# Expert order, the place of the split of x, and the copy of gather indices in a fused attention and MoE kernel

## The chip, the cores and the metric

One core of a Trainium2 chip runs the whole kernel as one program. The time is device time of one execution in microseconds (us).

## The reference

Attention with a compressive memory gives 2304 rows of 512 numbers (4 batches, 8 heads, 576 positions, head width 64). A mixture of experts with one expert for each row follows. What is computed, in short:

```python
local = softmax(causal(q @ k.T / 8)) @ v
mem_out = (phi(q) @ M_prev) / (phi(q) @ z_prev + 1e-6)        # phi(x) = elu(x) + 1
x = rows(g * mem_out + (1 - g) * local)                       # g = sigmoid(beta), 2304 x 512
logits = x @ w_gate                                           # 8 experts
expert_idx = argmax(logits, axis=1)                           # the first one of equal logits
gate_w = softmax(logits)[arange(2304), expert_idx]
for e in range(8):
    xe = x[expert_idx == e]
    out[expert_idx == e] = gate_w[...] * (relu(xe @ w1[e]) @ w2[e])   # 512 -> 1024 -> 512
```

## The kernel before

The program has two parts. The attention part (to about 262 us) writes the rows x with their gates to a scratch tensor in HBM; its order is fixed by a planner with costs and due times (the table `K`). The routing then sorts the row numbers by expert: `idx` holds 128 row numbers for each slot, `cnt` the number of full slots and of all slots of each expert position.

The MoE part works through slots. A slot is up to 128 rows of one expert. A position whose last slot has at most 64 rows runs it as a half slot, with 64 columns instead of 128; every position has at least one slot. `weight_unit` says which expert stands at position p: here p ^ 1, so the order is 1, 0, 3, 2, 5, 4, 7, 6. The router's weights (`wg_sw`) and the tie-break weights (`w8`, from an index operation in `consts`) are put in the same order.

Weights come as fp32 in 512 KB units, eight to an expert, by SyncE's queue into two stages. ScalarE makes the high fp16 part of a unit (`conv_hi`), VectorE the low part (`conv_lo`), into one of three buffers (position modulo 3). The conversions of later positions are spread over the slots, four units to a slot; `cuts` says how many of VectorE's four lie behind the first relu and behind the second, the rest behind the copy of xT: (1, 2) in a full slot, (0, 1) in a half one.

In each slot TensorE multiplies xT with w1 in two halves (`first_part`, m_ph, 96 matmuls in all), then with w2 (`second_part`, m_py, 24 matmuls in a full slot, 48 in a half one). Its code is one loop: for each of the three weight buffers i there is a block F{i} for a full slot and H{i} for a half slot, laid out F0, H0, F1, H1, F2, H2 with a few branches behind each (L1652 to L1656; `following`). L1654 leads to a full block of the next buffer, L1656 to a half one.

The rows of a slot come in four steps: GpSimd copies a column of `idx` (L1537) and issues an indirect gather of 128 rows into `xg` (L1489); VectorE splits them into a high and a low fp16 part `xn` (L1779 and L1782); SyncE issues two transposing DMAs into `xB` (L1410); VectorE copies xB to `xT` (L1793) when TensorE has read the old xT. Slot 0 is prepared in the routing, slot 1 has a gather of its own (`xg0`, semaphore g0) and is turned by TensorE. In before, the split for slot k stands at the start of VectorE's slot k - 1, ahead of the relus (L1750, L1752). VectorE, ScalarE, GpSimd and SyncE have loops of their own with unrolled branches for each state of the conversions; all wait on semaphores against registers.

Of the kernel before, what the change touches and what calls it, by code (L numbers as in the profile page):

```python
# [11 lines left out]
ALU = mybir.AluOpType  # L12
# [64 lines left out]

def weight_unit(w1, w2, p, u):

    e = p ^ 1  # L80
    if u < 4:
        return w1[e, 128 * u:128 * u + 128, :]
    return w2[e, 256 * (u - 4):256 * (u - 4) + 256, :].rearrange("(f p) d -> p f d", p=128)
# [18 lines left out]
def attention(nc, tc, es, q, k, v, M_prev, z_prev, beta, wg, w1, w2, x_dram, logits, mem, rout=None):  # L102
# [69 lines left out]
    def setup():  # L172
        wg_sb = const.tile([128, 4, 8], F32, name="wg_sb")
        nc.sync.dma_start(out=wg_sb, in_=wg.rearrange("(c p) e -> p c e", p=128))
        bt = const.tile([128, 8], F32, name="bt")
        nc.sync.dma_start(out=bt, in_=beta.rearrange("(o h) -> o h", o=1).to_broadcast([128, 8]))

        gm = const.tile([128, 8], F32, name="gm")
        gl = const.tile([128, 8], F32, name="gl")
        nc.scalar.activation(out=bt, in_=bt, func=AF.Tanh, scale=0.5)  # L180
        nc.vector.tensor_scalar(out=gm, in0=bt, scalar1=0.5 * SX, scalar2=0.5 * SX, op0=ALU.mult, op1=ALU.add)
        nc.vector.tensor_scalar(out=gl, in0=bt, scalar1=-0.5 * SX, scalar2=0.5 * SX, op0=ALU.mult, op1=ALU.add)

        wg_in, wg_sb = wg_sb, const.tile([128, 4, 8], F32, name="wg_sw")
        for i in range(2):
            nc.vector.tensor_copy(out=wg_sb[:, :, i::2], in_=wg_in[:, :, 1 - i::2])
        IW = const.tile([128, 4, 2, 72], F32, name="IW")
        nc.gpsimd.memset(IW, 0.0)
        for hh in range(2):
            r = slice(64 * hh, 64 * hh + 64)  # L190
            nc.vector.tensor_copy(out=IW[r, :, hh, 0:64], in_=ident[r, 64 * hh:64 * hh + 64].unsqueeze(1).to_broadcast([64, 4, 64]))
            nc.vector.tensor_copy(out=IW[r, :, hh, 64:72], in_=wg_sb[r])
        mz = xp.tile([128, 32, 64], F32, tag="xb", name="mz")
        early = xp.tile([128, 512], F32, tag="xt", name="early")
        zt = early[0:32, 256:384].rearrange("p (a d) -> p a d", a=2)
        for hh in range(2):
            nc.sync.dma_start(out=zt[:, hh], in_=z_prev.rearrange("b h d -> (b h) d"))
        mh = const.tile([128, 32, 73], F16, name="mh")
        ml = const.tile([128, 32, 73], F16, name="ml")
        nc.gpsimd.memset(ml[64:128], 0.0)  # L200
        T["gm"] = gm
        mw = early[:, 0:256].rearrange("p (i e) -> p i e", e=8)
        wgp = early[:, 384:512].rearrange("p (c m) -> p c m", c=4)
        nc.gpsimd.memset(wgp, 0.0)
        for hh in range(2):
            nc.vector.tensor_copy(out=wgp[64 * hh:64 * hh + 64, :, 8 * hh:8 * hh + 8], in_=wg_sb[64 * hh:64 * hh + 64])
        mt = xp.tile([128, 32, 64], F32, tag="xb", name="mt2").rearrange("p a d -> p (a d)")
        T.update(IW=IW, gl=gl, mh=mh, ml=ml, mz=mz, mw=mw, zt=zt, wgp=wgp, pws=mt[:, 1024:1536].rearrange("p (b a d) -> p b a d", b=4, a=2),
                 mt=mt[:, 0:1024].rearrange("p (c b d) -> p c b d", c=4, b=4))
# [769 lines left out]
NE = 8  # L979
# [9 lines left out]
class Routing:  # L989
# [25 lines left out]
    def consts(s):  # L1015
        V, G, kp = s.nc.vector, s.nc.gpsimd, s.tc.keep_in_program_order
        kp(G.memset(s.tri, 1.0))
        kp(G.affine_select(out=s.tri, in_=s.tri, pattern=[[1, 128]], compare_op=ALU.is_gt, fill=0.0, base=0, channel_multiplier=-1))
        kp(G.memset(s.ones, 1.0))
        kp(G.memset(s.cnt[:, NE:], 0))  # L1020
        kp(G.memset(s.idx[:, NS:NS + 1], 2303))
        kp(G.memset(s.ids[:, NS:NS + 1], 2304))
        ii = s.idx[:, 0:NS]
        it = s.tmp
        kp(G.iota(ii, pattern=[[128, NS]], base=0, channel_multiplier=0))
        kp(V.tensor_scalar(out=s.col, in0=ii, scalar1=BIG, scalar2=None, op0=ALU.add))
        kp(G.iota(it, pattern=[[-1, 128]], base=0, channel_multiplier=0))
        kp(V.tensor_copy(out=s.neg, in_=it))
        kp(G.iota(it[:, 0:NE].rearrange("p (a b) -> p a b", b=2), pattern=[[-2, NE // 2], [1, 2]], base=NE - 1, channel_multiplier=0))
        kp(V.tensor_copy(out=s.w8, in_=it[:, 0:NE]))  # L1030
        kp(G.iota(it[:, NE:2 * NE], pattern=[[128 * NJ, NE]], base=0, channel_multiplier=0))
        kp(V.memset(s.first, 0.0))
        kp(V.memset(s.less, 0.0))
        kp(V.memset(s.less[0:1, 0:1], -128.0))
        kp(V.tensor_copy(out=s.first[0:1], in_=it[0:1, NE:2 * NE]))
        tok = it[:, 16:34]
        for i in range(2):
            kp(G.iota(tok[:, 9 * i:9 * i + 8].rearrange("p (b t) -> p b t", t=4), pattern=[[576, 2], [128, 4]], base=1152 * i - 2304,
                      channel_multiplier=1))
            for a in range(2):  # L1040
                kp(G.iota(tok[64 * a:64 * a + 64, 9 * i + 8:9 * i + 9], pattern=[[0, 1]], base=512 + 576 * (2 * i + a) - 2304, channel_multiplier=1))
        kp(V.tensor_copy(out=s.vals, in_=tok))
# [181 lines left out]
def experts(nc, tc, es, x_dram, mem, rout, w1, w2, out):  # L1224
# [29 lines left out]
    with tc.tile_critical():  # L1254
        sems = {}
        for nm in ("h0", "h1", "y", "xh", "xl", "xc", "txh", "txl", "spw", "pw", "h0hi", "h0lo", "h1hi", "h1lo",
                   "ya", "gg", "g0", "cn", "fx", "px", "sc0", "sc1", "pa", "icp", "iscp", "chi", "clo",
                   "q0", "q1", "q0hi", "q0lo", "q1hi", "q1lo", "qy"):
            sems[nm] = es.enter_context(nc.semaphore("m_" + nm))
        wsem = [[es.enter_context(nc.semaphore(f"m_w{i}{u}")) for u in range(8)] for i in range(2)]  # L1260
# [228 lines left out]
            G.indirect_dma_start(out=x.rearrange("p h e -> p (h e)"), out_offset=None, in_=x_dram, in_offset=bass.IndirectOffsetOnAxis(ap=i, axis=0),  # L1489
                                 bounds_check=bound, oob_is_err=False).then_inc(S[sem], 16)  # L1490

        gather("g0", xg0, idx[:, 1:2])
        reg = {}

        for nm, x in (("g", 1), ("y", 0), ("c", 2), ("c1", 1), ("c2", NS), ("c3", 0), ("lim", 1)):
            reg[nm] = G.alloc_register(f"m_pool_{nm}")
            G.reg_mov(reg[nm], x)

# [23 lines left out]
        def scatter():  # L1522

            G.wait_ge(S["ya"], reg["g"])
            G.sem_inc(S["pa"], 1)
            send()

        def step():
            G.reg_mov(reg["c3"], reg["c2"])
            G.reg_mov(reg["c2"], reg["c1"])  # L1530
            G.reg_mov(reg["c1"], reg["c"])
            G.reg_add(reg["c"], reg["c"], 1)
            G.reg_add(reg["g"], reg["g"], 1)

        def turn():
            G.wait_ge(S["xl"], reg["g"])
            G.tensor_copy(out=ig, in_=idx[:, col("c")]).then_inc(S["icp"], 1)  # L1537
            G.wait_ge(S["icp"], reg["g"])
            G.sem_inc(S["pw"], 1)
            gather("gg", xg, ig)  # L1540
            scatter()
            step()
# [11 lines left out]
        G.reg_mov(reg["c"], NS)  # L1554
        turn()
        G.drain()
        scatter()
        step()

# [180 lines left out]
        for k in range(len(cs)):  # L1740
            if k > 0:
                V.wait_ge(S["cn"], k)
            cs[k]().then_inc(S["cn"], 1)
        rv = R(V, [(0, 1), (1, 1), (0, 16), (16, 16)])
        V.memset(ysb[:, 1], 0.0)

        def relu(i2, N, w, hi, lo):
# [8 lines left out]
            V.wait_ge(S[sem], 1)  # L1756

        relu(0, 128, once, "q0hi", "q0lo")
        V.wait_ge(S["g0"], 16)
        V.tensor_scalar(out=nat(xn[0]), in0=xg0[:, :, 0:64], scalar1=xg0[:, 7, 64:65], scalar2=None, op0=ALU.mult).then_inc(S["fx"], 1)  # L1760
        V.wait_ge(S["fx"], 1)
        V.scalar_tensor_tensor(out=nat(xn[1]), in0=xg0[:, :, 0:64], scalar=xg0[:, 7, 64:65], in1=nat(xn[0]),
# [5 lines left out]
        V.tensor_copy(out=xT[:, 1], in_=px[1]).then_inc(S["xc"], 1)  # L1768
        V.sem_inc(S["txl"], 16)

        def dve_body(rr, half, cv, nxt):
            N = 64 if half else 128

            def h(i2):
                relu(i2, N, rr.w, f"h{i2}hi", f"h{i2}lo")

            rr.w("txh", 0, 16)
            rr.w("gg", 0, 16)
            V.tensor_scalar(out=nat(xn[0]), in0=xg[:, :, 0:64], scalar1=xg[:, 7, 64:65], scalar2=None, op0=ALU.mult).then_inc(S["xh"], 1)  # L1779
            rr.w("txl", 0, 16)  # L1780
            rr.w("xh", 0, 1)
            V.scalar_tensor_tensor(out=nat(xn[1]), in0=xg[:, :, 0:64], scalar=xg[:, 7, 64:65], in1=nat(xn[0]),  # L1782
                                   op0=ALU.mult, op1=ALU.subtract).then_inc(S["xl"], 1)
            h(0)
            cuts = K["cuts"][half]
            for x in cv[:cuts[0]]:
                conv_lo(*x)
            h(1)
            for x in cv[cuts[0]:cuts[1]]:
                conv_lo(*x)  # L1790
            rr.w("txh", 16, 16)
            rr.w("txl", 16, 16)
            V.tensor_copy(out=xT, in_=xB).then_inc(S["xc"], 1)  # L1793
            for x in cv[cuts[1]:]:
                conv_lo(*x)
            rr.limits(nxt)
# [44 lines left out]
```

## Time and profile before

| | us |
|---|---|
| median of 3 runs | 503.66 |
| the runs | 499.33 to 504.02 |
| the profiled execution | 500.64 |
| its span, first to last instruction | 498.9 |
| TensorE busy in it | 462.2 |

The rows further down are from the profiled execution, in us from the start of its span. A row of the order of time has the start, the length, the engine, the line, the operation with its tiles and form, and the number of instructions; in brackets the idle time of the engine just before, and what ended it. "issue" is a wait for nothing that the profile shows. The ends of matmuls are modelled, so that rows of TensorE can overlap by some 0.15 us.

### The profile page before, as it was taken

How to read it: one execution, taken by the hardware profiler on the slowest of the kernel's cores; microseconds unless marked ns; L12 is line 12 of the kernel's file. 1: busy time of each engine (PE TensorE's matmuls, PEld its weight loads, DVE VectorE, ACT ScalarE, POOL GpSimd, SP SyncE). 2: the span in 40 equal slices, each digit the busy share in tenths (PEclk: the TensorE clock that was granted, in tenths of full speed). 3: DMA queues.
4: the chain of work that ended last, by engine and by line, in shares of the span. 5: the costliest groups of instructions: out<-in, count | busy, mean ns of one | idle time of the engine just before them, and what ended most of it. 6: DMA issues, size and time to landing. Idle time of an engine off the chain costs nothing.

```text
span 498.9 us, 14292 instructions
## 1 busy us (share of the span) xinstructions
PE 462.2 (93%) x5269; PEld 316.8 (64%) x5270; DVE 356.3 (71%) x785; ACT 221.7 (44%) x361; POOL 212.6 (43%) x395
## 2 busy tenths in 40 slices
PE   2999799999999989999989996999999999999795
PEld 0555356566666646657656774966777667777774
DVE  2788489787869647999885776898844588743682
ACT  3688465556666564557510443433300333300611
POOL 6567558367748344656231421232232122231132
PEclk9999799999999999999979999899999999999998
DMA  5567979899898989866148999799873459952332
GB/s 118 126 119 159 181 153 163 177 192 232 176 163 163 270 166 184 180 167 218 47 133 286 245 286 281 227 268 333 272 149 97 125 158 346 292 132 76 57 76 70
DMA packets 170106, 90.57 MB, mean 182 GB/s; under 512 B 151471, under 2 KB 152751, under 8 KB 170032
## 3 DMA queue, kind: packets, MB, share of 16 engines
q1 hardware_dynamic: 166192, 77.95, 67.2%
q0 software_dynamic: 3840, 11.80, 7.8%
q8 instruction: 26, 0.43, 0.4%
q14 instruction: 48, 0.39, 0.3%
HBM read 55.35 MB, written 11.60 MB: 134 GB/s over the span
## 4 chain that ended last, share of the span: by engine, by line
PE 60%; DVE 12%; DMA 10%; SPq 8%; issue 5%; ACT 2%; POOL 2%; DVEq 1%; POOLq 0%; ACTq 0%
PE m_ph L1581 17%; PE m_py L1597 13%; PE o L565 7%; PE st L491 5%; DMA m_xB<-m_xn 4%; SPq L275 3%; PE sm L596 3%; PE loc L677 3%; DMA m_xg<-x_scratch,m_ig 2%; PE sn L404 2%; SPq L277 2%; DMA QT<-mem 1%; PE m_py L1594 1%; PE wm L882 1%; DMA mem<-in_v_dram 1%
## 5 line engine op out<-in xcount | busy, mean ns | idle before, releaser
L1581 PE MATMUL m_ph<-m_xT,mem 128*128 128x128 f16 (+1 forms) x1344 | 68.8, 214 | 8.3 <-issue 4.3
L1581 PEld LDWEIGHTS m_ph<-m_xT,mem 128*128 128x128 f16 x1344 | 67.5, 100 | 12.2 <-issue 9.8
L412 DVE TENSOR_REDUCE mt<-sn 128x1 f32<-128x512 f32 (+4 forms) x83 | 54.4, 665 | 13.0 <-PE sn L410 10.7
L510 ACT ACTIVATE aT<-st 128x512 f32<-128x512 f32 x96 | 55.4, 594 | 18.4 <-PE st L491 18.0
L1710 ACT ACTIVATE m_y<-m_py 128x512 f32<-128x512 f32 x17 | 10.2, 597 | 117.0 <-PE m_py L1597 117.0
L495 POOL TENSOR_SCALAR_AFFINE_SELECT aT<-aT 128x128 f32<-128x128 f32 (+2 forms) x160 | 48.4, 320 | 32.3 <-ACT aT L510 30.3
L565 PE MATMUL o<-aT,mem 128*64 128x320 f32 (+4 forms) x320 | 59.2, 433 | 0.0
L1597 PE MATMUL m_py<-mem,m_hT 128*128 128x512 f16 x264 | 58.9, 379 | 0.0
L1750 DVE TENSOR_SCALAR m_hT<-m_ph 128x512 f16<-128x512 f32 (+1 forms) x46 | 29.0, 631 | 40.2 <-PE m_ph L1581 37.8
L1537 POOL COPY m_ig<-r_idx 128x1 int32 x22 | 4.1, 186 | 115.3 <-DVE m_xn L1782 114.3
L491 PE MATMUL st<-mem 128*128 128x64 f16 (+6 forms) x224 | 46.6, 262 | 0.4 <-ACT aL L532 0.2
L491 PEld LDWEIGHTS <-mem 128*128 128x128 f16 (+1 forms) x448 | 33.0, 99 | 16.3 <-issue 4.6
L1597 PEld LDWEIGHTS m_py<-mem,m_hT 128*128 128x128 f16 x264 | 25.3, 98 | 28.3
L491 PE MATMUL st<-QT,mem 66*128 66x64 f16 (+6 forms) x224 | 42.2, 262 | 0.4 <-ACT QT L455 0.4
L1581 PEld LDWEIGHTS m_ph<-m_xT,m_w 128*128 128x128 f16 x768 | 40.9, 98 | 1.8 <-issue 0.4
L1581 PE MATMUL m_ph<-m_xT,m_w 128*128 128x128 f16 (+1 forms) x768 | 41.6, 216 | 0.0
L1597 PE MATMUL m_py<-m_w,m_hT 128*128 128x512 f16 x168 | 37.4, 379 | 0.0
L565 PEld LDWEIGHTS o<-aT,mem 128*64 128x64 f32 x320 | 25.3, 137 | 16.7 <-issue 9.8
L1503 POOL DMA_INDIRECT out_dram<-m_y,m_is x23 | 25.5, 1109 | 20.1 <-POOL m_is L1509 18.0
L404 PE MATMUL sn<-mem 128*128 128x128 f16 (+3 forms) x158 | 31.4, 277 | 1.5 <-DVE mt L412 1.1
L1489 POOL DMA_INDIRECT m_xg<-x_scratch,m_ig x22 | 24.0, 1090 | 17.5 <-POOL m_ig L1537 17.5
L1275 DVE SCALAR_TENSOR_TENSOR mem<-mem,mem 128x1024 f16<-128x1024 f32 x24 | 28.6, 1218 | 2.5 <-ACT mem L1271 2.5
(257 smaller groups left out, 910.3 us busy)
## 6 DMA issues: line engine op xcount, KB each, us to landing
mem<-in_moe_w_dram SPq DMA_DIRECT2D x40, 512.0 KB, 6.0
m_stage<-in_moe_w_dram SPq DMA_DIRECT2D x24, 512.0 KB, 6.6
mem<-in_k_dram SPq DMA_DIRECT2D x32, 128.0 KB, 3.0
mem<-in_q_dram SPq DMA_DIRECT2D x32, 128.0 KB, 2.8
mem<-in_v_dram SPq DMA_DIRECT2D x32, 128.0 KB, 2.7
x_scratch<-xb SPq DMA_DIRECT2D x3, 1152.0 KB, 5.6
mem<-mem SPq DMA_DIRECT2D x6, 288.0 KB, 4.2
x_scratch<-xb SPq DMA_DIRECT2D x1, 864.0 KB, 3.8
```

Source lines behind the costliest of these rows:

```text
L404: nc.tensor.matmul(ps[:, c:c + k1 - k0], QT[:, 5 * hh + t, :], keys(hh)[:, k0:k1], start=(c == 0), stop=(k1 == parts[-1][3] and hh == part ...
L412: nc.vector.reduce_max(out, v, axis=AX.X)
L491: nc.tensor.matmul(ps[:, c:c + n], kk[:, kb, :], qq[:, w:w + n], start=(first and i == 0 and j == 0), stop=(last and i == 1 and j == len(p ...
L495: nc.gpsimd.affine_select(out=ap, in_=ap, pattern=pattern, compare_op=ALU.is_ge, fill=0.0, base=base, channel_multiplier=-1)
L510: nc.scalar.activation(out=a, in_=ps, func=AF.Exp, scale=ESC)
L565: nc.tensor.matmul(o[64 * hh:64 * hh + 64, q0:q0 + n], vv, aa, start=(j == 0), stop=(j == 4), skip_group_check=True)
L1275: V.scalar_tensor_tensor(out=W[e % 3][1][:, u], in0=stage[e % 2][u], scalar=SW, in1=W[e % 3][0][:, u], op0=ALU.mult, op1=ALU.subtract).the ...
L1489: G.indirect_dma_start(out=x.rearrange("p h e -> p (h e)"), out_offset=None, in_=x_dram, in_offset=bass.IndirectOffsetOnAxis(ap=i, axis=0) ...
L1503: G.indirect_dma_start(out=out, out_offset=bass.IndirectOffsetOnAxis(ap=i, axis=0), in_=ysb[:, j], in_offset=None, bounds_check=bound, oob ...
L1581: mm = PE.matmul(ph[i2][:, f, 0:N], w[:, kc, c:c + 128], x[:, j, kc, 0:N], start=(i == 0), stop=(i == 11), skip_group_check=True)
L1597: mm = PE.matmul(py, hh, ww[:, 4 + ff // 2, c:c + 512], start=st, stop=sp_)
L1750: V.tensor_scalar(out=hT[i2][0][:, :, 0:N], in0=ph[i2][:, :, 0:N], scalar1=0.0, scalar2=None, op0=ALU.max).then_inc(S[hi], 1)
```

## The change

Three things. The expert at position p becomes (p + 1) % 8, so the order is 1, 2, 3, 4, 5, 6, 7, 0; the router's columns and the tie-break weights follow (two copies of 7 and 1 columns, one more index operation). VectorE's split of x moves from the start of a slot to right behind the copy of xT, and is that of the slot behind the next: the split for slot k + 2 stands behind the copy for slot k + 1, in VectorE's slot k, ahead of the rest of the conversions. One split stands ahead of the loop, and GpSimd issues one gather more at the end. GpSimd copies the index column as soon as the gather before has landed (gg), ahead of the wait for the split (xl); the gather of slot 1 now counts on the same semaphore gg.

```diff
 def weight_unit(w1, w2, p, u):
-    e = p ^ 1
+    e = (p + 1) % 8
...
-        for i in range(2):
-            nc.vector.tensor_copy(out=wg_sb[:, :, i::2], in_=wg_in[:, :, 1 - i::2])
+        nc.vector.tensor_copy(out=wg_sb[:, :, 0:7], in_=wg_in[:, :, 1:8])
+        nc.vector.tensor_copy(out=wg_sb[:, :, 7], in_=wg_in[:, :, 0])
...
-        kp(G.iota(it[:, 0:NE].rearrange("p (a b) -> p a b", b=2), pattern=[[-2, NE // 2], [1, 2]], base=NE - 1, channel_multiplier=0))
+        kp(G.iota(it[:, 0:NE], pattern=[[-1, NE]], base=NE - 1, channel_multiplier=0))
+        kp(G.iota(it[:, NE - 1:NE], pattern=[[0, 1]], base=NE, channel_multiplier=0))
...
-        gather("g0", xg0, idx[:, 1:2])
+        gather("gg", xg0, idx[:, 1:2])
...
         def turn():
-            G.wait_ge(S["xl"], reg["g"])
+            G.wait_ge(S["gg"], reg["g16"])
+            G.sem_inc(S["pw"], 1)
             G.tensor_copy(out=ig, in_=idx[:, col("c")]).then_inc(S["icp"], 1)
             G.wait_ge(S["icp"], reg["g"])
+            G.wait_ge(S["xl"], reg["g"])
             G.sem_inc(S["pw"], 1)
             gather("gg", xg, ig)
             scatter()
...
         turn()
         G.drain()
+        G.wait_ge(S["xl"], reg["g"])
+        G.sem_inc(S["pw"], 1)
+        gather("gg", xg, ig)
         scatter()
...
+        def x_split(wait):
+            V.tensor_scalar(out=nat(xn[0]), in0=xg[:, :, 0:64], scalar1=xg[:, 7, 64:65], scalar2=None, op0=ALU.mult).then_inc(S["xh"], 1)
+            wait()
+            V.scalar_tensor_tensor(out=nat(xn[1]), in0=xg[:, :, 0:64], scalar=xg[:, 7, 64:65], in1=nat(xn[0]),
+                                   op0=ALU.mult, op1=ALU.subtract).then_inc(S["xl"], 1)
+
+        V.wait_ge(S["gg"], 32)
+        x_split(lambda: once("xh"))
+
         def dve_body(rr, half, cv, nxt):
...
-            rr.w("txh", 0, 16)
-            rr.w("gg", 0, 16)
-            V.tensor_scalar(out=nat(xn[0]), in0=xg[:, :, 0:64], scalar1=xg[:, 7, 64:65], scalar2=None, op0=ALU.mult).then_inc(S["xh"], 1)
-            rr.w("txl", 0, 16)
-            rr.w("xh", 0, 1)
-            V.scalar_tensor_tensor(out=nat(xn[1]), in0=xg[:, :, 0:64], scalar=xg[:, 7, 64:65], in1=nat(xn[0]),
-                                   op0=ALU.mult, op1=ALU.subtract).then_inc(S["xl"], 1)
             h(0)
...
             V.tensor_copy(out=xT, in_=xB).then_inc(S["xc"], 1)
+            rr.w("gg", 32, 16)
+            x_split(lambda: rr.w("xh", 1, 1))
             for x in cv[cuts[1]:]:
                 conv_lo(*x)
```

Not shown: the register g16 (16, then 16 more in each pass), the registers of VectorE for the new waits, and the semaphore g0 that goes.

## Rows read from the trace of the kernel before

**Rows 1.** Who waited for whom, TensorE alone, from 262 us: total, times, longest

```profile
PE m_ph L1581 <- issue: 5.8, 2, 4.3
```

**Rows 2.** Order of time, TensorE: first parts of slots 3, 4 and 5

```profile
295.69 5.52 PE L1581 MATMUL m_ph<-m_xT,mem 128*128 128x128 f16 x96 [0.48 <-DVE m_xT L1793]
...
310.67 4.51 PE L1581 MATMUL m_ph<-m_xT,mem 128*128 128x64 f16 x96 [4.28 <-issue]
...
317.96 5.52 PE L1581 MATMUL m_ph<-m_xT,m_w 128*128 128x128 f16 x96
```

**Rows 3.** Stretches: length, busy us (instructions) of each engine, granted clock, DMA, GB/s

```profile
0.00:262.00 262.00, 240.69 (x2381) 149.49 (x2382) 197.50 (x560) 152.34 (x276) 149.85 (x302) 0.97 0.79 166
...
310.60:313.00 2.40, 2.33 (x53) 2.36 (x54) 1.24 (x3) 2.12 (x3) 0.01 (x1) 0.63 0.09 32
```

**Rows 4.** TensorE's branches L1656 and L1654: ns min/median/max, first and last start

```profile
L1656 PEldq COMPARE_BRANCH  x3: 169/169/6614, 303.9 to 486.0; - x3
...
L1654 PEldq COMPARE_BRANCH  x7: 67/209/233, 303.7 to 485.9; - x7
```

**Rows 5.** Instruction queues (q8 TensorE's) in 0:262, 262:304, 304:310.6, 330:462: packets, MB, share

```profile
q8 instruction: 18, 0.29, 0.5%
...
q8 instruction: 3, 0.05, 0.5%
...
q8 instruction: 1, 0.02, 0.9%
...
q14 instruction: 17, 0.14, 0.4%
```

**Rows 6.** Order of time, TensorE: slots 12, 13, 18, 19, 20 and 22

```profile
391.73 5.52 PE L1581 MATMUL m_ph<-m_xT,mem 128*128 128x128 f16 x96
...
402.27 5.52 PE L1581 MATMUL m_ph<-m_xT,mem 128*128 128x128 f16 x96
...
454.97 3.27 PE L1581 MATMUL m_ph<-m_xT,mem 128*128 128x64 f16 x96
...
461.06 2.97 PE L1581 MATMUL m_ph<-m_xT,m_w 128*128 128x64 f16 x96
...
470.05 5.52 PE L1581 MATMUL m_ph<-m_xT,mem 128*128 128x128 f16 x96 [3.10 <-DVE m_xT L1793]
...
487.23 2.96 PE L1581 MATMUL m_ph<-m_xT,mem 128*128 128x64 f16 x96 [0.32 <-DVE m_xT L1793]
490.35 3.06 PE L1594 MATMUL m_py<-mem,m_hT 128*64 128x256 f16 x48 [0.16 <-DVE m_hT L1750]
```

**Rows 7.** Order of time, VectorE: split of slot 1, slot 2's split and copy, slot 3's split

```profile
268.17 0.49 DVE L1760 TENSOR_SCALAR m_xn<-m_xg 128x512 f16<-128x512 f32 x1 [0.89 <-DMA m_xg<-x_scratch,r_idx]
...
274.06 0.49 DVE L1779 TENSOR_SCALAR m_xn<-m_xg 128x512 f16<-128x512 f32 x1 [1.26 <-DMA m_xg<-x_scratch,m_ig]
...
282.30 0.43 DVE L1793 COPY m_xT<-m_xB 128x1024 f16<-128x1024 f16 x1 [0.23 <-DMA m_xB<-m_xn]
...
284.92 0.48 DVE L1779 TENSOR_SCALAR m_xn<-m_xg 128x512 f16<-128x512 f32 x1
```

**Rows 8.** Order of time, VectorE: conversion and copy ahead of slot 20, split at 488.51

```profile
467.46 1.23 DVE L1275 SCALAR_TENSOR_TENSOR mem<-mem,mem 128x1024 f16<-128x1024 f32 x1 [2.50 <-ACT mem L1271]
469.48 0.43 DVE L1793 COPY m_xT<-m_xB 128x1024 f16<-128x1024 f16 x1 [0.79 <-DMA m_xB<-m_xn]
...
488.51 0.49 DVE L1779 TENSOR_SCALAR m_xn<-m_xg 128x512 f16<-128x512 f32 x1 [1.43 <-DMA m_xg<-x_scratch,m_ig]
```

**Rows 9.** Order of time, ScalarE: the four conversions in slot 12 and in slot 19

```profile
395.59 3.90 ACT L1271 ACTIVATE m_w<-mem 128x1024 f16<-128x1024 f32 x4 [2.92 <-issue]
...
466.37 3.90 ACT L1271 ACTIVATE mem<-mem 128x1024 f16<-128x1024 f32 x4 [4.20 <-issue]
```

**Rows 10.** Order of time, SyncE's first weight loads; GpSimd's first gather of the loop

```profile
262.55 7.32 SPq L1383 DMA_DIRECT2D mem<-in_moe_w_dram  x8
...
265.87 1.03 POOL L1489 DMA_INDIRECT m_xg<-x_scratch,m_ig  x1 [0.80 <-POOL m_ig L1537]
```

More of the change, by code (lines that the diff above doesn't have):

```diff
@@ L1256, in experts @@
         for nm in ("h0", "h1", "y", "xh", "xl", "xc", "txh", "txl", "spw", "pw", "h0hi", "h0lo", "h1hi", "h1lo",
-                   "ya", "gg", "g0", "cn", "fx", "px", "sc0", "sc1", "pa", "icp", "iscp", "chi", "clo",
+                   "ya", "gg", "cn", "fx", "px", "sc0", "sc1", "pa", "icp", "iscp", "chi", "clo",
                    "q0", "q1", "q0hi", "q0lo", "q1hi", "q1lo", "qy"):
@@ L1490, in gather @@
                                  bounds_check=bound, oob_is_err=False).then_inc(S[sem], 16)
-        gather("g0", xg0, idx[:, 1:2])
+        gather("gg", xg0, idx[:, 1:2])
         reg = {}
-        for nm, x in (("g", 1), ("y", 0), ("c", 2), ("c1", 1), ("c2", NS), ("c3", 0), ("lim", 1)):
+        for nm, x in (("g", 1), ("y", 0), ("c", 2), ("c1", 1), ("c2", NS), ("c3", 0), ("lim", 1), ("g16", 16)):
             reg[nm] = G.alloc_register(f"m_pool_{nm}")
@@ L1533, in step @@
             G.reg_add(reg["g"], reg["g"], 1)
+            G.reg_add(reg["g16"], reg["g16"], 16)
         def turn():
-            G.wait_ge(S["xl"], reg["g"])
+            G.wait_ge(S["gg"], reg["g16"])
+            G.sem_inc(S["pw"], 1)
             G.tensor_copy(out=ig, in_=idx[:, col("c")]).then_inc(S["icp"], 1)
             G.wait_ge(S["icp"], reg["g"])
+            G.wait_ge(S["xl"], reg["g"])
             G.sem_inc(S["pw"], 1)
@@ L1743, in experts @@
             cs[k]().then_inc(S["cn"], 1)
-        rv = R(V, [(0, 1), (1, 1), (0, 16), (16, 16)])
+        rv = R(V, [(0, 1), (1, 1), (16, 16), (32, 16)])
         V.memset(ysb[:, 1], 0.0)
@@ L1758, in experts @@
         relu(0, 128, once, "q0hi", "q0lo")
-        V.wait_ge(S["g0"], 16)
+        V.wait_ge(S["gg"], 16)
         V.tensor_scalar(out=nat(xn[0]), in0=xg0[:, :, 0:64], scalar1=xg0[:, 7, 64:65], scalar2=None, op0=ALU.mult).then_inc(S["fx"], 1)
```

## The prediction

> **What bounds the kernel now.** I read the waits of TensorE first, from the routing's end (262 us) on, because the diff leaves the attention part alone but for one 8-column index operation on GpSimd. The largest entry there is "issue" [rows 1]: TensorE stood still and the profile shows nothing that it waited for. TensorE's order of time says where. From 317.96 to 454.97 us blocks follow each other without an idle row, 10.54 us to a full slot (391.73 to 402.27) [rows 2, 6]; whatever the change does to other engines in that stretch is hidden unless it breaks this cover. The idle time sits at the two ends: 0.48 us ahead of slot 3 and 4.28 us ahead of slot 4 [rows 2], 3.10 us ahead of slot 20, 0.32 and 0.16 us in slot 22 [rows 6]. So those five places are read one by one.
>
> The 4.28 us is a branch. Slot 4 is a half block, expert position 1, and the program goes from the full block of buffer 0 (F0) to the half block of buffer 1 (H1) by line 1656. That branch took 6614 ns once, at 303.9 us, and 169 ns otherwise; line 1654, which leads to a full block, never took over 233 ns [rows 4]. The queue that carries instructions to TensorE explains it: up to 262 us it made 18 refills of 0.29 MB while 4763 matmuls and weight loads ran [rows 3, 5], so one refill, 16 KB, holds some 260 instructions (estimate: 4763 / 18 = 265). Three more came from 262 to 304, one inside the idle time, none from 330 to 462 [rows 5]. The blocks lie in the order F0, H0, F1, H1, F2, H2; a full one has 120 matmuls and as many weight loads (240), a half one 288. F0 + H0 + F1 are 768, three refills; H1 is the next piece, and had to be fetched with TensorE standing still. [...]
>
> **Experts move up.** Both orders begin with expert 1. With the reference's inputs the router gives experts 0 to 7 the token counts 2, 465, 120, 834, 36, 680, 12, 155, so (full slots, H for half) the order before is 4 | H | 7 | 1 | 5+H | H | 1+H | H and the order after 4 | 1 | 7 | H | 5+H | H | 1+H | H: 23 slots both times, 18 full and 5 half. Only slots 4 and 12 trade places. Before, slot 4 took 306.23 (295.69 + 10.54) to 317.96 = 11.73 us and slot 12 took 10.54, together 22.27. After, slot 4 runs F1, which is loaded by the count above: 10.54, with no stop and so no loss of clock; slot 12 is a half slot, 6.09 us as 454.97 to 461.06 [rows 6]. Together 16.63: **-5.64 us**. If F1 is not there, the stop and the slow clock stay (+5.6).
>
> Two new prices come with it. At the end of slot 4 the program now branches from F1 over H1 to F2, where it ran straight from H1 into F2 before. The refills for that stretch start while F1 runs and have its second part, 10.54 - 5.52 = 5.0 us, against 4.28 us for the one fetched without cover. From 0 to 4.28 + 1.55 us; I take **0**, as the later switches are 169 to 233 ns [rows 4].
>
> Slot 12 as a half slot has its first conversion ahead of the copy of xT (`cuts`), and that conversion needs ScalarE's high part. ScalarE starts it at 395.59, after 2.92 us of "issue" behind the eviction [rows 9], and this comes from code before the slot, so it stays. One of the four takes 0.98, then VectorE 1.23 and the copy 0.43: copy done 398.23, TensorE starts 0.14 later (469.91 to 470.05), 6.64 us after 391.73 against a length of 6.09: a stall of 0.56. The other half slot of this kind, 19, took 461.06 to 470.05 = 8.99, of which VectorE's wait for a DMA is 0.79 (the copy's row at 469.48) [rows 6, 8]: 8.20 - 6.09 = 2.1. I take **+1.0**, nearer to the first, since that is this very place, with two more branches on the way to half-slot code.
>
> Copying the two router columns in pieces of 7 and 1 instead of 4 and 4 is two instructions for two; the extra index operation lies in the attention part, away from TensorE's waits. Both cost nothing.
>
> **The split of x behind the copy.** Before, VectorE makes copy, two conversions, split (282.30, then 284.92) [rows 7]; after, copy, split, conversions. The work per slot is the same, and the removed waits on the transposes were met already. What moves is the start of transpose, gather and the next split, by some 2.2 us. Place by place:
> - Slot 3: the transposes behind the split wait in the same queue as four weight loads issued ahead of them, so of 0.48 us I take **-0.3** (0 to -0.48).
> - Slot 20: its 3.10 us wait is for the copy at 469.48. The conversion ahead of that copy ends at 467.46 + 1.23 = 468.69 and waited for ScalarE, whose 4.20 us of "issue" ahead of 466.37 [rows 8, 9] the change does not touch; only the 0.79 us wait for the transposes behind it goes. **-0.79** (as far as -3.1 if ScalarE's stop goes too).
> - Slot 22: its split sat behind two conversions of 1.2 and would start some 2.4 us earlier; the 0.32 us wait for the copy goes. The gather it then asks for lands earlier too, so the 1.43 us wait at 488.51 [rows 8] that pushed the relu behind TensorE goes, and with it 0.16. **-0.48** (0 to -0.48).
>
> **Index copied ahead of the wait.** It takes about 1 us out of the loop split - gather - split, which no TensorE wait outside those above hangs on. But the first pass now waits for the first gather to land (VectorE starts on it at 268.17 [rows 7]) where the second gather left at 265.87 [rows 10]. So that gather leaves 3.3 us later (268.17 and some 1 us for the index copy). Its cover is the weight loads: SyncE issued eight of them from 262.55 to 269.87 [rows 10], the transposes of slot 2 go through the same queue behind those whether they are issued at 275 or 278, and the copy's end (282.73) is some 1.8 us ahead of slot 2 (295.69 - 0.48 - 10.54 = 284.67). Without that cover 3.3 - 1.8 = 1.5. I take **0**. One gather and one split are added behind the last slot; TensorE, the last eviction and the last scatter do not wait for them: 0.
>
> **Sum**: -5.64 + 0 + 1.0 - 0.3 - 0.79 - 0.48 + 0 = -6.2 us. The profiled execution took 500.64 (span 498.9 and 1.7 around it), so it would be 494.4, a ratio of 0.988. The median of the three runs, 503.66, lies 0.6% above the profiled one; by the same ratio it becomes **497.4 us**, my forecast.
>
> [...] Of the trace: the backward switch of buffers, F2 to F0 at 391.73, shows no idle time and no refill [rows 5, 6], so pieces from 262 us on stay loaded. [...]
>
> **Rivals.**
> - *The stop stays at slot 4* (the three refills do not reach F1; for it: the count is exact, with no room for the code around the blocks). Slot 4 then pays 4.28 + 1.55 again: 500.2 on the profiled run, 503.2 on the median. Chance 0.2.
> - *The hidden part is all there is*: slot 12's stall is 2.1 and more, ScalarE's and VectorE's own code stops move into the open (VectorE's code gets shorter, so all its branches move), and half the gain is lost: about 497.5, or 500.5. Speaks for it: ScalarE's rows already have such stops of 2.92 and 4.20 us [rows 9]. Chance 0.12.
> - *Slower*: two forward branches, over H0 and over H1, where there was one stop before. If a block that was jumped over keeps the next from being loaded, slots 4 and 5 both pay 4.28 + 1.55; slot 4's gain is gone and slot 5 is new: 494.4 + 5.8 + 5.8 = 506.0, or 509 on the median. It decides as soon as line 1654 takes over about 5 us twice. Against it: refills went on from 262 to 304 while only F0 ran. Chance 0.1. The gathers do not make it slower by themselves: the first of the loop landed at 274.0 after 8.1 us [rows 7, 10], and a split may start some 3 us behind the copy before the next relu holds up TensorE (slot 2's second part at 284.67 + 5.52, less two conversions, the split and one relu, some 4.4 us together: 285.8, against the copy's end at 282.73).
> - The forecast: 0.58.
>
> **Range and chances.** The bounds of the forecast alone: 494.4 with 2.3 to 3 us of luck (slot 20, slot 12) is 491.5; with slot 12 and slot 5 at their worse ends it is 498 to 500. Its own range is 491 to 500.5. To reach the first rival I go to 504; the slower rival stays out. 1%, some 5 us, is about what a measurement of this kernel tells from no change (its three runs spread over 4.7 us). The forecast is 6.2 us, not far above: four fifths of its chance, and a little of the second rival, are faster, 0.5; the slower rival alone is slower, 0.1; the rest, 0.4, is within 1%.
>
> **What the profile after would show.** Slot 4 with 128x128 blocks and no idle row ahead of it, line 1656 without a long branch, the granted clock at full there; slot 12 with 64-column blocks, and an idle row of 0.5 to 2 us ahead of slot 13; slot 20's wait down to about 2.3 us with ScalarE's stop still ahead of its conversions; the splits right behind the copies at L1793; the second gather at about 269 us and slot 2 without a wait. I am wrong if a refill sits in an idle gap of TensorE at slot 4 or 5, or if VectorE waits for gathers long enough that relus come late.

## The result, and the profile after

The change made the kernel faster by 0.9%: median 499.5 us (496.3 to 505.8, 15 runs) beside 503.38 us of the kernel before, ratio 0.9911 (95% interval 0.9883 to 0.9939). Run again beside other kernels it came to 0.9977 (0.9941 to 1.0013), so the gain is small and near what a measurement can tell. Ratios compare undisturbed runs only, so they can differ a little from a quotient of medians.

The profiled execution after took 499.99 us (span 498.2), against 500.64 (498.9) before: hardly a gain in this pair. Its slot 0 starts 1.07 us earlier (261.91 against 262.98 us), ahead of all that was meant to change; in the 14 traces of this study that start lies anywhere from 259.80 to 266.29 us. So lengths below are counted from slot 0's start to the end of the span: 235.9 us before, 236.3 after. This execution lies at the median after (499.99 beside 499.5), the one before 2.7 us under its own (500.64 beside 503.38); so the pair of traces cannot show the gain of the medians, and where the timed runs have it is not read from this pair.

TensorE's waits from 262 us on after the change (total, times, longest), beside [rows 1]:

```profile
PE m_ph L1588 <- issue: 6.0, 4, 3.6
PE m_ph L1588 <- DVE m_xT L1802: 3.1, 3, 2.2
```

The largest is again "issue" (1.49 us of it stand ahead of slot 0, as 1.53 us do before). TensorE's order of time after, slots 3, 4 and 5, then 12 and 13, then 19, 20 and 22, which answers to [rows 2, 6]:

```profile
295.81 5.52 PE L1588 MATMUL m_ph<-m_xT,mem 128*128 128x128 f16 x96 [0.43 <-DVE m_xT L1802]
...
310.06 7.15 PE L1588 MATMUL m_ph<-m_xT,mem 128*128 128x128 f16 x96 [3.56 <-issue]
...
322.23 5.52 PE L1588 MATMUL m_ph<-m_xT,m_w 128*128 128x128 f16 x96
...
396.01 2.96 PE L1588 MATMUL m_ph<-m_xT,mem 128*128 128x64 f16 x96
...
404.04 5.52 PE L1588 MATMUL m_ph<-m_xT,mem 128*128 128x128 f16 x96 [2.19 <-DVE m_xT L1802]
...
465.41 0.78 PE L1588 MATMUL m_ph<-m_xT,m_w 128*128 128x64 f16 x21 [0.52 <-issue]
...
469.88 5.52 PE L1588 MATMUL m_ph<-m_xT,mem 128*128 128x128 f16 x96 [0.52 <-DVE m_xT L1802]
...
486.79 2.97 PE L1588 MATMUL m_ph<-m_xT,mem 128*128 128x64 f16 x96
```

The orders did trade: slot 4 has 128x128 blocks, slot 12 has 128x64. But slot 4 still stops, 3.56 us, and its first part takes 7.15 us instead of 5.52, for the granted clock is 0.50 of full speed from 310.1 to 313 us, where it was 1.00 in the idle time ahead (stretches: length, busy us of each engine, granted clock, DMA share, GB/s; compare [rows 3]):

```profile
306.50:310.10 3.60, 0.04 (x2) 0.07 (x2) 1.61 (x2) 2.34 (x3) 2.56 (x3) 1.00 1.32 229
310.10:313.00 2.90, 2.90 (x29) 2.90 (x30) 0.00 (x0) 2.15 (x3) 0.00 (x0) 0.50 1.10 169
```

The long branch is now the one to a full block (ns min/median/max), beside [rows 4], and TensorE's queue made one refill from 264.5 to 303 us where the kernel before made two:

```profile
L1661 PEldq COMPARE_BRANCH  x7: 67/209/6009, 303.9 to 485.9; - x7
...
q8 instruction: 1, 0.02, 0.2%
```

From slot 3's start to slot 5's plus slot 12: 26.42 + 8.03 = 34.45 us, against 22.27 + 10.54 = 32.81 before. Slot 13 waits 2.19 us for the copy; behind ScalarE's stop of 4.30 us come conversion and copy (order of time, ScalarE and VectorE, beside [rows 9]):

```profile
401.24 3.90 ACT L1272 ACTIVATE m_w<-mem 128x1024 f16<-128x1024 f32 x4 [4.30 <-issue]
...
402.33 1.23 DVE L1276 SCALAR_TENSOR_TENSOR m_w<-mem,m_w 128x1024 f16<-128x1024 f32 x1 [1.58 <-ACT m_w L1272]
403.47 0.42 DVE L1802 COPY m_xT<-m_xB 128x1024 f16<-128x1024 f16 x1
403.81 0.48 DVE L1779 TENSOR_SCALAR m_xn<-m_xg 128x512 f16<-128x512 f32 x1
```

The last line is the moved split, right behind the copy. At the other end slot 20 waits 0.52 us instead of 3.10, and slot 22 no longer waits; slots 19 and 21 have new stops for "issue", 0.52 and 0.47 us.

### The profile page after: what moved, and what is told of

It reads as the page before. It is cut to its first block, busy times and chain, and to the rows that moved or that the text cites. A ratio compares the mean times of both kernels' runs of the same rounds, so it can differ in the third digit from the quotient of the medians.

```text
span 498.2 us, 14273 instructions
## 1 busy us (share of the span) xinstructions
PE 462.2 (93%) x5269; PEld 316.2 (63%) x5270; DVE 354.3 (71%) x787; ACT 221.0 (44%) x361; POOL 216.8 (44%) x397
## 4 chain that ended last, share of the span: by engine, by line
PE 68%; DMA 8%; DVE 7%; issue 6%; SPq 5%; ACT 2%; POOL 1%; POOLq 0%; ACTq 0%; DVEq 0%
PE m_ph L1588 18%; PE m_py L1604 14%; PE o L565 9%; PE st L491 7%; PE sm L596 3%; PE loc L677 3%; PE sn L404 3%; SPq L275 2%; DMA m_xB<-m_xn 2%; PE m_py L1601 2%; DMA m_xg<-x_scratch,r_idx 1%; DMA QT<-mem 1%; SPq L277 1%; DMA m_xg<-x_scratch,m_ig 1%; PE mem L631 1%
## 5 line engine op out<-in xcount | busy, mean ns | idle before, releaser
L1490 POOL DMA_INDIRECT m_xg<-x_scratch,m_ig x23 | 27.1, 1180 | 94.6 <-DVE m_xn L1781 67.5
L1759 DVE SCALAR_TENSOR_TENSOR m_hT<-m_ph,m_hT 128x512 f16<-128x512 f32 (+1 forms) x46 | 29.1, 633 | 1.6
L683 POOL TENSOR_TENSOR xb<-lt,xb 128x288 f32<-128x288 f32 x28 | 23.6, 846 | 12.4 <-DVE lt L680 8.1
```

The source lines that it names most:

```text
L1759: V.scalar_tensor_tensor(out=hT[i2][1][:, :, 0:N], in0=ph[i2][:, :, 0:N], scalar=0.0, in1=hT[i2][0][:, :, 0:N], op0=ALU.max, op1=ALU.subtr ...
```

## The experiments

Their expectations call F0, H0, F1, H1, F2, H2 the blocks of TensorE's loop; "order alone" is the expert order without the split's move and without the index copy ahead.

**One part at a time.** The order alone takes of the change only this (with the router's columns and the tie-break weights):

```diff
-    e = p ^ 1
+    e = (p + 1) % 8
```

> The kernel before with the experts' order alone moved up (copies of router columns and tie-break weights with it); the split and the index copy stay where they were. Theory A (the stop of TensorE's code stays at slot 4, since the piece that holds F1 is asked for only when slot 3 ends; slot 12's half slot brings a stall ahead of slot 13): slot 4 waits 3 to 4.5 us for 'issue' ahead of it, line of the branch to a full block up to 6 us once, slots 4 and 12 together 21.5 to 22.5 us, a stall of 1 to 2.2 us ahead of slot 13; ratio to the kernel before 1.000 to 1.005 (0 to +2.5 us). Rival B (the order is the gain, as the prediction had it; the one profile after was a bad draw): no 'issue' ahead of slot 4, -3.5 to -5 us, ratio 0.990 to 0.993.

Median 496.97, ratio 0.9906 (0.9861 to 0.9951). Theory A fell on the time. Its trace (499.69 us, above most of its 12 runs, 490.93 to 500.9) shows what theory A said: 3.66 us of "issue" ahead of slot 4, 1.64 us ahead of slot 13, 235.5 us from slot 0 on.

The complement puts that line back and keeps the rest:

```diff
-    e = (p + 1) % 8
+    e = p ^ 1
```

> The change with the experts' order put back as it was; the split stands behind the copy, the index copy ahead of the wait. Theory A (the gain is the split's: slot 20 gains 2.6 us, slot 22 0.5, slot 3 up to 0.5): ratio 0.991 to 0.995 (-2.5 to -4.5 us), slot 4 still stops about 4 us, no stall ahead of slot 13, slot 20 waits about 0.5 us. Rival B (the order is the gain): ratio 0.997 to 1.000, slot 20's wait about 2.3 us.

Median 501.41, ratio 1.0019 (0.9980 to 1.0057); 4.65 us at slot 4 (H1), 1.19 us ahead of slot 3, 0.65 ahead of slot 20. So the order brings the gain, and split and index copy bring none. The medians by themselves, beside 499.65 for the kernel before in this group, say the same with half the size: 0.9946 and 1.0035.

**Where the code lies.** Nothing but the number of warm-up matmuls ahead of the loop's code differs, two instructions for each (the diffs of the table `K`, here and further on, show a part of its line):

```diff
-wu=5, wv=0, w3=36
+wu=5, wv=0, w3=60
```

> The changed kernel with 24 more warm-up matmuls of 64 columns ahead of the loop's code, nothing else: the loop's blocks start 48 instructions further into a piece of code. Theory A (a piece is asked for when the one before it is entered; F0's end lies 2 to 5 instructions short of the next piece, so F1's piece is asked for only at slot 3's end; with the shift F0's end lies in it and F1's piece is there before slot 4): no 'issue' ahead of slot 4, granted clock there at full, slot 4 10.5 us, -4.5 to -6 us against the changed kernel, ratio to the kernel before 0.979 to 0.983. Rival C (the stop comes from the jump itself, or from the weight transfers' load on the queues, wherever the code lies): the stop stays, ratio 0.990 to 0.993 as the changed kernel.

> The kernel before with the same 24 warm-up matmuls more. H1 lies one piece further than F1. Theory A: with the shift F1's piece is asked for early but H1's is not, so the jump from F0 to H1 at slot 4 still stops for 3 to 5 us; ratio 0.998 to 1.002. Rival D (the shift is worth something by itself, warm-up or alignment of any block): no stop at slot 4 or time elsewhere, ratio 0.988 to 0.992. Rival C gives 1.000 too.

With the shift the changed kernel's slot 4 starts without a wait, and 231.0 us pass from slot 0 to the end, 5.3 less than in the trace after. The kernel before keeps its stop, 3.55 us. That was theory A's claim for the traces. The times do not bear it out: the changed kernel shifted has a ratio of 0.9971 (0.9933 to 1.0009), where theory A had 0.979 to 0.983, and no lower than unshifted in its own comparisons (0.9911, 0.9977). Not foreseen, the kernel before, which kept the stop, came to 0.9966 (0.9933 to 0.9999); 232.8 us pass in its trace from slot 0 on, 3.1 less than before, 2.8 of them at slot 20, which waits 0.29 us instead of 3.10. Whether the place of the code or the warm-up matmuls themselves brought that was not separated.

The changed kernel again:

> The changed kernel again, for a second trace and beside the order alone on one chip. Theory F (the gain is the order's: the stop at slot 4 is there in some executions and absent in others, since the end of F0's block lies at the border of two pieces of code; the split is worth nothing, -1 to +1 us): ratio to the kernel before 0.988 to 0.994, and a trace either with 3.5 us of 'issue' at slot 4 and some 498 us of span, or with none and 491 to 494 us. Rival A (the stop is always there and the gain is the split's): the stop again; the split alone was already 1.002, so this rival would need the split to be worth something only together with the order.

This trace has no stop at slot 4: two refills from 264.5 to 303 us, the second at about 298 us. TensorE's slots 3 to 5 in it:

```profile
297.88 7.15 PE L1588 MATMUL m_ph<-m_xT,mem 128*128 128x128 f16 x96 [1.98 <-DVE m_xT L1802]
...
310.04 5.52 PE L1588 MATMUL m_ph<-m_xT,mem 128*128 128x128 f16 x96
...
322.09 4.68 PE L1588 MATMUL m_ph<-m_xT,m_w 128*128 128x128 f16 x81 [1.34 <-DVE m_w L1276]
328.29 1.01 PE L1588 MATMUL m_ph<-m_xT,m_w 128*128 128x128 f16 x15 [1.51 <-issue]
```

```profile
q8 instruction: 2, 0.03, 0.3%
...
L1661 PEldq COMPARE_BRANCH  x7: 67/209/4207, 307.2 to 486.3; - x7
```

So the same program stops in one execution and not in another. But this execution, at 500.78 us, is the slowest of its 12 runs, and 235.9 us passed all the same: 1.98 us of wait and a slow first part at slot 3, 1.34 us ahead of slot 5 and 1.51 of "issue" in it took the place of the stop.

The profile puts the 1.34 us down to a conversion of weights. Its end (321.94 us) coincides with that of a long branch, the 4.21 us of the jump to slot 5 (317.72 to 321.93), which ended 1.46 us behind the landing of a refill, as the long branches at slot 4 do in all seven traces with a stop there (1.4 to 1.5 us). In the trace of the changed kernel without the index copy (below) such a branch ended 0.2 us behind the conversion named, so its 1.56 us there are a wait for code; here the two cannot be told apart.

The order alone, shifted on and shifted back:

```diff
-wu=5, wv=0, w3=36
+wu=5, wv=0, w3=60
...
-wu=5, wv=0, w3=36
+wu=5, wv=0, w3=26
```

> The order alone, with 24 more warm-up matmuls of 64 columns ahead of the loop's code (48 instructions). Theory F: F1's piece is always there at slot 4, no 'issue' ahead of it; ratio 0.983 to 0.989, a stall of about 1.6 us ahead of slot 13. Rival G (the order's gain does not come from slot 4, and the warm-ups cost up to 1 us): 0.990 to 0.994.

> The order alone, with 10 warm-up matmuls fewer (20 instructions): F0's end lies 15 to 20 instructions short of the border, so its piece's successor can't be entered before slot 3 ends. Theory F: the stop of 3.5 us at slot 4 and the slow clock behind it in every execution; ratio 0.999 to 1.006. Rival G: 0.988 to 0.993, as the order without this.

Shifted on: no stop at slot 4, 231.0 us from slot 0 on, median 493.95, ratio 0.9931 (0.9898 to 0.9965): the trace is what theory F expected, the time what rival G did. Shifted back: the stop as expected (3.78 us), one refill, but a ratio of 1.0212 (1.0164 to 1.0259), far over both theories. Most of that is at the end, TensorE's slots 20 and 22, and its queue's refills from 460 to 500 us (the first line of counts; the second is that of the order unshifted, from 460 us to its end):

```profile
468.04 0.27 PE L1582 MATMUL m_ph<-m_xT,mem 128*128 128x128 f16 x2 [3.03 <-DVE mem L1276]
470.83 8.28 PE L1582 MATMUL m_ph<-m_xT,mem 128*128 128x128 f16 x94 [2.52 <-issue]
...
492.99 4.51 PE L1582 MATMUL m_ph<-m_xT,mem 128*128 128x64 f16 x96 [2.95 <-issue]
```

```profile
q8 instruction: 8, 0.13, 1.4%
```

```profile
q8 instruction: 1, 0.02, 0.2%
```

By 20 instructions the loop's start slipped over a border (it lies two matmuls into F0, where slot 20 stops), and code that had stayed loaded was fetched again. The run says nothing, then, on what the stop at slot 4 costs in time.

**The cuts.** The shifted order with the half slot's copy ahead of all conversions:

```diff
-cuts=((1, 2), (0, 1))
+cuts=((1, 2), (0, 0))
```

> The order alone with the 24 warm-up matmuls and, in half slots, all four of VectorE's conversions behind the copy of xT (cuts (0, 0) instead of (0, 1)). The copy no longer waits for ScalarE's conversion: no wait ahead of slot 13 (1.6 us before) nor ahead of slot 20 beyond the transposes (0.5 to 1 us less); -1.5 to -2.5 us against the same kernel without the cut, ratio 0.979 to 0.985 if the stop is gone too. Rival: the conversion made later holds up TensorE at the weights of a later slot, and the wait moves there: no difference.

Median 496.49, ratio 0.9964 (0.9930 to 0.9997), 2.5 us above the same kernel without the cut. The rival was right in that nothing is gained, but not on the place: the copy now waits for its transposes (2.13 us), slot 13 still waits 0.90, and the relus behind the conversions hold up the second parts of slots 13 and 20 by 0.88 and 0.89 us.

**The index copy.** The change without its third part, in GpSimd's `turn`:

```diff
-            G.wait_ge(S["gg"], reg["g16"])
-            G.sem_inc(S["pw"], 1)
+            G.wait_ge(S["xl"], reg["g"])
             G.tensor_copy(out=ig, in_=idx[:, col("c")]).then_inc(S["icp"], 1)
             G.wait_ge(S["icp"], reg["g"])
-            G.wait_ge(S["xl"], reg["g"])
```

> The changed kernel without its third part: GpSimd waits for the split, then copies the index column, as in the kernel before, and the gather of slot 1 has its own semaphore again; the split stays behind the copy. Theory H (the split's part costs because the first pass now waits for the first gather to land: the second gather left at 269.7 to 270.5 us instead of 264 to 265.5, and the copies of xT for slots 2 and 3 come late): the second gather about 5 us earlier, no wait ahead of slots 2 and 3, 1 to 2 us less than the changed kernel, ratio 0.988 to 0.992 as the order alone. Rival J (the cost comes from the split's place on VectorE, which pushes conversions back): 0.994 to 0.998, waits ahead of slots 2 and 3 as before.

And the suspected wait by itself, in the kernel before:

```diff
+        G.wait_ge(S["g0"], 16)
         G.wait_ge(S["cn"], 7)
```

> The kernel before with one wait more: GpSimd waits once, ahead of its loop, for the first gather to land. This is the suspected cost by itself. Theory H: the second gather 4 to 5 us later, VectorE's split for slot 2 at 276 to 278 us instead of 274, relus of slot 1 late, waits ahead of slot 2 or 3; +1 to +2 us, ratio 1.002 to 1.005. Rival J: no difference, 0.999 to 1.001.

The first: ratio 0.9863 (0.9790 to 0.9937), from six runs; the second gather left at 265.03 us and slot 2 did not wait, but slot 3 did, 1.07 us, which theory H had excluded. The second: 0.9989 (0.9952 to 1.0025). Its trace shows the late gather (order of time, GpSimd; compare [rows 10]) and a relu that holds up TensorE by 1.20 us in slot 1:

```profile
269.50 1.03 POOL L1489 DMA_INDIRECT m_xg<-x_scratch,m_ig  x1 [0.80 <-POOL m_ig L1537]
...
278.65 5.34 PE L1598 MATMUL m_py<-mem,m_hT 128*128 128x512 f16 x24 [1.20 <-DVE m_hT L1751]
```

The time shows none of it. Theory H is not borne out, and the two runs leave open what the index copy is worth.

**Further on.** The blocks 118 instructions on, by warm-ups in smaller pieces:

```diff
-wu=5, wv=0, w3=36
+wu=40, wv=0, w3=60
...
-            busy(K["wu"])
+            busy(K["wu"], 64)
```

> The order alone, with the loop's blocks 118 instructions further on (24 warm-up matmuls of 64 columns more, and five of 512 columns made as forty of 64: the same columns). Theory F, carried on: the 0.8 to 1.6 us of 'issue' ahead of slot 5 are the piece that holds F2, asked for when F1 crosses a border 63% into its block; now the border lies 35% into it, so neither slot 4 nor slot 5 stops; 1 to 2.5 us less than with the shift of 48, ratio 0.987 to 0.991. Rival K (the jump over H1 costs that much wherever the code lies): the wait ahead of slot 5 stays, 0.992 to 0.994.

> The order and the split behind the copy, without the index copy ahead, with the blocks 118 instructions further on: all that the runs so far speak for. By theories F and H no stop at slots 4 and 5, no wait ahead of slots 2 and 3, 1.5 to 2 us ahead of slot 13, 0.5 to 1.2 ahead of slot 20: ratio 0.983 to 0.990. If the split is worth nothing by itself, the same as the order alone so laid out; if rival J holds, 1 to 1.5 us more than that.

Both missed: 0.9947 (0.9912 to 0.9981) and 0.9972 (0.9932 to 1.0012). The jump to F1 no longer stops, but 41 matmuls into F1 TensorE does, and again 22 matmuls into F2. TensorE's slots 4 and 5, order alone, 118 on:

```profile
306.97 2.45 PE L1582 MATMUL m_ph<-m_xT,mem 128*128 128x128 f16 x41
311.76 3.23 PE L1582 MATMUL m_ph<-m_xT,mem 128*128 128x128 f16 x55 [2.34 <-issue]
...
320.01 1.39 PE L1582 MATMUL m_ph<-m_xT,m_w 128*128 128x128 f16 x22
322.06 4.30 PE L1582 MATMUL m_ph<-m_xT,m_w 128*128 128x128 f16 x74 [0.66 <-issue]
```

The same place in slot 5, order alone, 48 on, and then the change without the index copy, not shifted:

```profile
314.52 3.35 PE L1582 MATMUL m_ph<-m_xT,m_w 128*128 128x128 f16 x57
318.64 2.35 PE L1582 MATMUL m_ph<-m_xT,m_w 128*128 128x128 f16 x39 [0.78 <-issue]
```

```profile
318.40 4.68 PE L1585 MATMUL m_ph<-m_xT,m_w 128*128 128x128 f16 x81 [1.56 <-DVE m_w L1276]
323.63 1.01 PE L1585 MATMUL m_ph<-m_xT,m_w 128*128 128x128 f16 x15 [0.55 <-issue]
```

81, 57 and 22 matmuls for shifts of 0, 48 and 118 instructions: at two instructions to a matmul (it and its weight load) the steps of 24 and 35 are the shifts' 48 and 70. The stop sits at a fixed count of instructions from the program's start, wherever the padding puts the block: the border of a piece of code.

## Why the prediction was right, and where it was not

**Direction and size.** Forecast -6.2 us on the profiled execution; measured -0.9%, about 4.5 us of 503, and less in the second comparison; of the median 497.4 us was forecast and 499.5 measured. To see which part carries it, all runs of the change's own comparison and of the kernels of the first two groups except the one shifted back were put into one least-squares fit, with a level for each group and one term for each edit: the order -3.5 us (95%: 1.0 either way), split and index copy together +1.4 (0.9), the shift of 48 -1.2 (1.0), the cuts +2.3 (1.7). The last two are near what such a fit can tell. The prediction had -5.64 + 1.0 = -4.6 for the order and -1.57 for the rest. So the order's term has its sign and most of its size, and the rest the wrong sign. That the total came so near is in part luck: the slot 4 on which the sum rests came in one of the two traces of the changed kernel, and that one was the slowest of its runs.

**"slot 4 runs F1, which is loaded by the count above"** is the step that failed as it stood. Three refills did come by 304 us in the trace before, and the order of the blocks was right; but what sets off a refill was left out, and only two came by then in the trace after. The traces fit this: a piece is asked for when TensorE's sequencer enters the one before it. A piece is 256 instructions by an estimate: the stops 41 matmuls into F1 and 22 into F2 in the trace of the order alone 118 on lie 158 + 288 + 44 = 490 matmuls and weight loads and some 22 other instructions apart, two pieces by the prediction's 265. Counted in the program as built, in steps of 256 from the borders that slots 4 and 5 showed, F0's loop branch is the first instruction of a piece, and F1 begins in the next. Slot 0 runs code of its own ahead of F0, so slot 1 is the first to reach that branch. The times of the refills agree: the one that F1's start needs began in slot 1, at 279.1 to 281.8 us, in all four traces shifted by 48; unshifted it began in slot 1 twice (281.8, 282.2 us), in slot 3 twice (296.9, 298.1), and in three traces not before the jump to slot 4. The table has every trace by what slot 4 runs and by the shift:

| slot 4 runs | shift | traces | refills 264.5 to 303 us | stop at the jump to slot 4, us |
|---|---|---|---|---|
| F1 | -20 | 1 | 1 | 3.78 |
| F1 | 0 | 4 | 1, 1, 2, 2 | 3.56, 3.66, none, none |
| F1 | +48 | 3 | 2 each | none |
| F1 | +118 | 2 | 2 each | none; 2.34 and 0.84 later in the block |
| H1 | 0 | 3 | 2, 1, 2 | 4.28, 4.65, 3.54 |
| H1 | +48 | 1 | 2 | 3.55 |

With the border behind F0's end (-20) the piece came too late; shifted by 48 and by 118 it came in time; on the border (0) it went either way. H1 lies further on, and the jump to it stopped in all four traces. The first rival ("the stop stays at slot 4", 500.2 us for the profiled execution) is what the trace after shows, with 499.99 us; the forecast's slot 4 is what the second trace shows. The prediction's sum took one of two outcomes, and its first rival, at 0.2, the other. How often each comes in the timed runs no trace can say.

The refills at the loop's end are in line with the same count. Counted from the border that the stop two matmuls into F0 shows, the loop (1584 matmuls and weight loads, and some branches) lies on seven pieces unshifted and on eight shifted back; in the traces of the order alone the queue made one refill from 460 us on unshifted, and eight shifted back. That the eighth piece is the reason is an inference from these two traces.

**What the stop is worth.** The prediction priced it at 4.28 + 1.55 us, the 1.55 being 4.51 less 2.96, the first parts of slots 4 and 22 before [rows 2, 6]. The stop and the slow clock were there at that size (3.56 + 1.63). In traces its absence is worth that: slot 5 begins 54.8 us behind slot 0 in the changed kernel shifted, 60.3 us in the trace after. But in the second trace after, waits in slots 3 to 5 took it all back, and the kernel before, shifted, took 232.8 us from slot 0 on with its stop, against 231.0 in the two best traces without one. The timed runs do not show it. The order shifted on has a median 3 us below the order as it is, on different chips, and by ratio it is no better (0.9931 beside 0.9906). A further term in the fit, for shift and new order together, comes to +1.2 us (1.9): the shift does no more for the kernels whose stop it removes than for the one that keeps it. So that the order gains is shown, and that it gains by slot 4 is not. Either few of the timed runs stop there, or the gain lies elsewhere; the part ahead of slot 0, whose end differs by 6.5 us between traces, was not timed by itself.

**Slot 12 to 13, +1.0.** Mis-sized: 2.19 us, just above its upper bound of 2.1. The chain was the one named, conversion behind ScalarE's stop, then the copy, but the stop was 4.30 us, not the 2.92 of [rows 9]. In the traces with the new order, the old split and the old cuts it was 3.2 to 3.4 us and slot 13 waited 1.15 to 1.64; with both edits it was 3.9 to 4.3 and the wait 1.81 to 2.19. Why the split's place makes ScalarE's stop longer was not tried.

**Branch from slot 4 to 5, 0.** In the two unshifted traces of the new order with a stop at slot 4 there was none at slot 5; without one, 0.55 to 3.85 us of "issue" inside slot 5. So part of the stop is put off to the next border, up to 2.9 us in the second trace after if the wait ahead of slot 5 is counted. The upper bound, 4.28 + 1.55, held.

**Slot 3, -0.3.** Wrong: all kernels with the split behind the copy except one wait ahead of slot 2 or 3 (0.43, 1.98, 1.19, 0.94 and 1.07 us), and none of the five shown with the new order and the old split does (the kernel before had 0.48). By an estimate from these waits, half of the +1.4 of split and index copy can be this and half slot 13. How the moved split makes the copies of slots 2 and 3 late is not shown; seen is only that VectorE's conversions now come behind it.

**Slot 20, -0.79.** The wait fell by 2.58 us, near the end "if ScalarE's stop goes too"; that stop was 3.12 us instead of 4.20. It is not the change's: the kernel before, shifted, waits 0.29 there with a stop of 2.50, and the kernel before with the extra wait 3.06 with one of 4.58. A term read from one execution was a draw.

**Slot 22, -0.48**: as predicted in the trace after. **The late second gather, 0**: it left 4.6 us later. With the wait alone put into the kernel before, one trace shows a cost of 1.20 us in slot 1, within the bound of 1.5, and the time shows none (0.9989).

**The third rival** (slots 4 and 5 both stop) did not happen in full in any trace. The lowest median of the study is the order alone, shifted by 48: 493.95 against 497.68 for the changed kernel in the same group. Beside the kernel before, three others have ratios as low (0.9863, 0.9906, 0.9911, against 0.9931) with intervals that overlap, so which is best stays open.

## What to carry to other kernels

Where an engine runs a loop of large blocks, look at where each block begins and ends against the pieces in which code is fetched, not only at how many pieces there are: 20 instructions of padding fewer ahead of the loop cost this kernel more (ratio 1.0212) than the edit under study gave. A stop read from one trace is a draw, so take a second trace before it becomes a term. A step moved on a busy engine to start earlier can push back what stood there: the moved split, with the index copy, was to save 1.6 us and cost 1.4.

## What was not expected of the hardware

A jump to code that was not there took 6.0 to 7.1 us by the record of its branch, in the seven traces with a stop at slot 4 (6.01 in the trace after, 6.61 in the one before), though one refill is only 16 KB (18 of them 0.29 MB [rows 5]). In the trace after, 3.5 us passed until the refill began, 1.1 until it had landed and 1.4 until the branch ended; TensorE's matmuls still to be done hid some 2.4 us. From a block's first matmul to the use of the next piece, its run to the border plus the stop there, 2.1 to 6.2 us passed (1.39 + 0.66 to 4.68 + 1.51); the jump itself lies earlier, as the sequencer runs ahead of the matmuls (in the trace after it reached the jump at 303.9 us, and the matmuls of slot 3 ended at 306.5). A stop in the middle of a block can be told from a wait for data by its place: the same instruction in each run, moved by exactly the padding (81, 57 and 22 matmuls into F2 for 0, 48 and 118 instructions). And idle time of TensorE did not always make the first part behind it longer: behind 1.98 us ahead of slot 3 (second trace after) it took 7.15 us; behind 2.19 us ahead of slot 13 (first trace) it took 5.52, at a granted clock of 1.00.
